# Attention and a long convolution mixed by a gate: when VectorE's lesser work may begin, the normalisation in three pieces, and other places for two sets of loads

## The chip, the core and the metric

The kernel runs on one core of one Trainium2 chip. The metric is device microseconds from the launch to the end of the program. Three engines matter here. TensorE (PE in the profile) multiplies, ScalarE (ACT) takes exponentials, VectorE (DVE) does everything else. SyncE (SP) issues nearly all transfers. Each engine works through its own queue strictly in the order in which the program wrote it, and waits on semaphores where an operand is not there yet.

## The reference

```python
def reference(A_x, A_wqkv, A_wo, B_u, B_A_re, ..., B_log_dt, B_Dskip, gate_w):
    g = sigmoid((x * gate_w).sum(-1, keepdims=True))
    # a: attention, 32 heads of 16, sequence 2048, no mask
    q, k, v = (x @ wqkv) split in heads
    a = softmax(q @ k.T * 16 ** -0.5) @ v @ wo
    # b: a diagonal state-space layer, 512 channels of 128 complex states
    K[d, l] = real(sum_n C[d, n] * exp(dt * A[d, n] * l) * dt * B[d, n])
    b = causal_convolution(x, K) + x * Dskip
    return g * a + (1 - g) * b          # (1, 2048, 512), bfloat16
```

## The kernel before

**The attention.** A block is four heads and a quarter of the queries (512), so there are 32 blocks, 0 to 31. A block has 16 key tiles of 128 keys, and each gives four score tiles, one for each head: 2048 score tiles of 128 keys by 512 queries in all. They are handled in 683 *groups* of three. The groups are numbered from 0 here, and group n is the n-th long ScalarE instruction `ET<-SC`. For each group TensorE multiplies `SC<-Qm,KT` into one of two score buffers (`SC0`, `SC1`, in turn), and ScalarE takes the exponential of it into seats of `ET`, a ring of 15 tiles. TensorE then multiplies these with the values (`OA<-ET,VE`).

**VectorE's share of the exponentials.** In some groups ScalarE takes only two of the three tiles. VectorE makes the third from the bits of a scaled score (`bits`, `DZ<-SC`). Four such tiles make a *set*, which is one key tile of four heads; 64 sets make 256 tiles. A set also needs two more VectorE steps over all four tiles, `DU<-DZ` and later `DZ<-DZ` in place, with products `OA<-DZ,VE`, `OA<-DU,VS` and `OA<-DZ,VS` between them. A block may only end once its sets' products are in.

**The end of a block.** `norm_a` transposes `OA` into `OT`. `norm_b` (one pair of blocks at a time) takes the reciprocal `Rz`, from block 24 on multiplies it by the gate `gq`, and multiplies it into `ON`. `norm_c` transposes `ON` into `OnT`, which the output product needs.

**The convolution** runs beside it, in pieces on VectorE and TensorE: tables of powers (`tt`, `PT`), the convolution's near part (`kstage`, `Kst`), states for each chunk of 64 steps (`sstage`, `SG`, marks S0 to S15 for its 16 channel blocks), a scan over the chunks, and 32 units of `y` (`ystage`, unit u marks `yu{u}`). A y unit reads `Py` and `Tt`, which `yload` fetches, and `XY`, which `xload` fetches. Its result goes through DRAM and comes back transposed as `Yl`. At the end `outs` adds `Yl` to the gated attention of the first three quarters, in three additions `AR<-AR,Yl`, and stores them. The last quarter goes through TensorE: `first` and the closing lines multiply `Yl` with the identity and `OnT` with `Wo` into one accumulator.

**The order.** A scheduler inside the kernel (`Sched`) decides in which order the instructions of each queue are written. Each piece of work is a thread that yields segments: an engine, a cost, and a rank `up`, where a smaller rank goes first. After each group, `fill(until, pe_until, want)` picks segments whose inputs it believes ready before `until`, the believed end of that group's exponential. Segments with rank -1 or -2 are those for which others wait at once: `bits`, `norm_a`, the emptying of the accumulator `MB`. On TensorE, `want` asks for a least amount of multiplying. Where real work does not reach it, products with zeros are written (`<-wm`). `force` pulls work ahead of its turn where a group cannot go on without it, for instance where the exponentials need a seat in `ET` that an earlier product still reads. For VectorE the only test of time before the change is this one (`e` is the believed start):

```python
                elif e > until:
                    continue
```

Every matmul is recorded in one helper, so the profile gives all of them line 626. Tiles tell them apart.

Of the kernel before, what the change touches and what calls it, by code (L numbers as in the profile page):

```python
# [18 lines left out]
T = 64  # L19
# [18 lines left out]
SGH = 256  # L38
SGAT = (175, 315)
SMM = .058  # L40
XS = 128 * DH ** -.5 / math.log(2)
STEP = ((42, 205 / 256), (84, 166 / 256))
XB = 128 * (127 - math.log2(3.15037))
# [236 lines left out]
class Sched:  # L280
# [89 lines left out]
    def fill(self, until, pe_until, want=0):  # L370
        while True:
            best = None
            for t in self.thr:
                e = self.est(t)
                if e is None:
                    continue
                if t.eng == "PE":
                    own = sum(a[2].get("a", 0) for a in t.seg if isinstance(a, tuple))
                    room = max(0, want - self.p.act - own) * ZCOL
                    if e + t.cost + room > pe_until and t.up > 0 or e > min(until, pe_until):  # L380
                        continue
                elif e > until:
                    continue
                now = self.p.tm[t.eng]
                k = (max(e, now + .3) if e > now + .02 else now, t.up, t.n)
                if best is None or k < best[0]:
                    best = (k, t)
            if best is None:
                return
            self.issue(best[1])  # L390
# [22 lines left out]
def declare(nc, es):  # L413
    B = {}

    def sb(name, free, dt=BF16):
        B[name] = Buf(name, "sb", free, dt)
# [83 lines left out]
        sb(f"X2{k}", 1024)  # L501
        sb(f"XY{k}", 32 * 64)

    sb("Py", 3 * 2 * 16 * T)
    sb("Tt", 3 * 8 * 64)
    sb("Yst", 4 * 256)
    sb("XR", 2 * 1024)
    for i in range(2):
# [101 lines left out]
def record(nc, p, B, ins):  # L610
# [369 lines left out]
    def norm_b(b, n=1):  # L980
        w = b % 2 + 1 - n
        at, ks = (lambda o, d, k: OT(512 * w + o, ([[512, 2]] if n == 2 else []) + d)), range(w, w + n)
        two = [[16, 2]] if n == 2 else []
        op("DVE", lambda v: v.reciprocal(Rz(16 * w, two + [[1, 16]]), at(16, [[32, 16]], 0)), [(OT, k, b - n + 1 + k - w) for k in ks],
           [(Rz, k) for k in ks], c=.25)
        if b >= 24:
            gq = B["gq"]
            op("DVE", lambda v: v.tensor_tensor(Rz(16 * w, two + [[1, 16]]), Rz(16 * w, two + [[1, 16]]), gq(0, ([[0, 2]] if n == 2 else []) + [[1, 16]]), ALU.mult),
               [(Rz, k) for k in ks] + [(gq, j) for j in range(4)], [(Rz, k) for k in ks], c=.11)
        op("DVE", lambda v: v.tensor_tensor(ON(16 * w, two + [[32, 16], [1, 16]]), at(0, [[32, 16], [1, 16]], 0),  # L990
                                            Rz(16 * w, two + [[1, 16], [0, 16]]), ALU.mult),
           [(OT, k, b - n + 1 + k - w) for k in ks] + [(Rz, k) for k in ks], [(ON, k) for k in ks], c=.08 + .267 * n)
# [290 lines left out]
    def sstage(blk):  # L1283
# [8 lines left out]
        for bank in range(4):  # L1292
            yield ("LOCK", "MB")
            kh, part = bank % 2, bank // 2
            for k0 in range(0, 8, 4):
                yield ("PE", 4 * SMM)
                for k in range(k0, k0 + 4):
# [3 lines left out]
                       [(Qt, (blk % 2, 2 * part + kh), blk)] + [(X2[blk % 4], 0, blk)], [(MB, 0, ('S', blk, bank))],  # L1301
                       c=SMM, a=64)
            yield ("DVE", .65, -1)
# [48 lines left out]
    Py, Tt, Yst, ytd, Yl = B["Py"], B["Tt"], B["Yst"], B["ytd"], B["Yl"]  # L1352
# [2 lines left out]

    def yload(u):
        blk, hf = divmod(u, 2)
        r = u % 3
        yield ("SP", .5)
        dma("SP", lambda e: e.dma_start(Py(r * YN, [[16 * T, 2], [1, 16 * T]]),  # L1360
                                        ptd.dram(blk * P * PTN + hf * 16 * T, [[PTN, P], [CB * T, 2], [1, 16 * T]])),
            [(ptd, blk)], [(Py, r, u)], c=.62, lat=3.8)
        for par in range(2):
            for a in range(2):
                yield ("SP", .4)
                dma("SP", lambda e, par=par, a=a: e.dma_start(
                    Tt(r * 512 + 256 * a, [[64, 4], [1, 64]], 64 * par, 64),
                    kpd.dram(blk * P * 8 * P + (2 * hf + a) * 40 * 8 * P + par * 9 * P, [[1, 64], [18 * P, 4], [1, 64]])),
                    [(kpd, blk)], [(Tt, (r, par, a), u)], c=.64, lat=2.8)
        sch.mark(f"yl{u}")  # L1370

    def yloads():
        yield ("AFTER", "S12")
        for u in range(2 * NBLK):
            if u >= 3:
                yield ("AFTER", f"yu{u - 3}")
            yield from yload(u)

    def ystage():
        def unit(u):  # L1380
            blk, hf = divmod(u, 2)
            qr, bl = divmod(blk, 4)
            sg, h, k8 = SG[qr // 2], qr // 2, blk % 8
            r, r2 = u % 3, u % 4
            yield ("AFTER", f"scan{h}")
            yield ("AFTER", "gt")
            yield ("AFTER", f"yl{u}")
# [84 lines left out]

    def xyloads():
        for qr in range(4):
            yield ("AFTER", f"yu{8 * qr - 5}" if qr else "S12")
            yield from xload(B[f"XY{qr}"], qr)
            sch.mark(f"xy{qr}")

# [35 lines left out]
    def wo_load(b):  # L1514
        load("SP", b, lambda: dap(ins["wo"], 0, [[D, P], [P * D, 4], [1, D]]), [(b, 0)], [[D, 4], [1, D]])
# [43 lines left out]
    def outs():  # L1559
        for blk in range(NBLK):  # L1560
            yield ("AFTER", f"yr{blk}")
        for qc in range(3):
            AO = B[f"AR{qc}"]
            yield ("DVE", 2.3, 0)
            op("DVE", lambda v, qc=qc, AO=AO: v.tensor_tensor(AO(0, [[D, 4]] + NAT), AO(0, [[D, 4]] + NAT), Yl(4 * D * qc, [[D, 4]] + PERM), ALU.add),  # L1565
               [(AO, r, "a") for r in range(4)] + [(Yl, x) for x in range(NBLK)], [(AO, r, "y") for r in range(4)], c=2.2)
            later("SP", .5, 3, lambda qc=qc, AO=AO: dma("SP", lambda e: e.dma_start(dap(ins["out"], 512 * qc * D, [[D, P], [P * D, 4], [1, D]]), AO(0, [[D, 4], [1, D]])),
                                                        [(AO, r, "y") for r in range(4)], [(B["d_out"], qc)], c=.5, lat=3))
        yield ("SP", .5)
        wo_load(B["Wo"])  # L1570
        sch.mark("outs")

    def projs():
# [28 lines left out]
    def norms():  # L1602
        for b in range(31):
            yield ("AFTER", f"end{b}")
            yield ("DVE", .75, -2)
            norm_a(b)
            sch.mark(f"n{b}")
            if b == 30:
                yield ("DVE", .65, 1)
                norm_b(b)  # L1610
            if b % 2 == 1:
                yield ("DVE", .9, 1)
                norm_b(b, 2)
                yield ("DVE", .7, 1)
                norm_c(b)
                sch.mark(f"c{b}")
# [93 lines left out]
    for g in range(NG):  # L1710
# [8 lines left out]
        if g + 1 < NG:  # L1719
# [5 lines left out]
            while lack >= 256 and bare:  # L1725
                n = 512 if lack >= 512 else 256
# [10 lines left out]
        t = p.tm["ACT"]  # L1737
# [5 lines left out]
        while lack >= 256 and p.tm["PE"] < t + OVER:  # L1743
# [4 lines left out]
            n = 512 if lack >= 512 else 256  # L1748
# [11 lines left out]
    ahead_of(1)  # L1760
    ahead_of(2)
    norm_a(31)
    norm_b(31)
    for k in range(2):
        norm_c(31, k, 2)
        for i in (2 * k, 2 * k + 1):
# [3 lines left out]
    for i in range(4):  # L1770
        b, off, sl = banks[i]
# [40 lines left out]
```

## Time and profile before

| | us |
|---|---|
| median of 3 runs | 840.84 (839.78 to 841.8) |
| the profiled execution | 841.1 |
| its span, first to last instruction | 839.3 |
| ScalarE busy | 818.9 (98%) |
| VectorE busy | 788.4 (94%) |
| TensorE busy | 696.9 (83%) |

ScalarE is busy nearly all the time. A group's exponential and the idle time ahead of it are the rows to read. In the timeline, a bracket at the end of a row holds the engine's idle time before the row and the instruction that ended it. The granted clock is the share of TensorE's full clock, 1.00 or 0.50 here.

### The profile page before, as it was taken

To read this page: it belongs to the slowest core of one execution; us is meant where nothing else is said; L and a number is where in the kernel's file an instruction comes from. 1 tells how busy PE (TensorE), PEld (TensorE's weight loads), DVE (VectorE), ACT (ScalarE), POOL (GpSimd) and SP (SyncE) were. 2 spreads that over 40 slices of the span, in tenths; PEclk is the share of its full clock that TensorE was granted. 3 is DMA by queue.
4 is the path that set the end of the run, shared out by engine and by line. 5 is a ranking of instruction groups with operands and counts; after the bars stand their busy time and mean duration, and the time that the engine had idled before them with its cause. 6 is when DMAs were issued, how large, how long until landed. Compare 5 with 4: busy or idle time off the path is not lost.

```text
span 839.3 us, 21027 instructions
## 1 busy us (share of the span) xinstructions
PE 696.9 (83%) x8977; PEld 253.4 (30%) x9002; DVE 788.4 (94%) x1344; ACT 818.9 (98%) x695; POOL 11.0 (1%) x13
## 2 busy tenths in 40 slices
PE   7787777778778888887787888789887889999987
PEld 3232332222212333332232332244432223444322
DVE  5799999998899999999999999999999989999996
ACT  7999999999999999999999999999999999999986
POOL 4000000000000000000000000000000000000000
PEclk9999999998999999999999999999999999999989
DMA  9650044792450789983392692066664025555113
GB/s 206 148 78 11 23 76 98 198 228 56 135 174 5 213 108 219 138 207 65 137 149 38 97 176 46 1 146 164 168 147 125 4 74 112 124 131 135 28 40 98
DMA packets 247954, 94.91 MB, mean 113 GB/s; under 512 B 222644, under 2 KB 234804, under 8 KB 245812
## 3 DMA queue, kind: packets, MB, share of 16 engines
q1 hardware_dynamic: 245988, 92.51, 50.1%
q10 hardware_dynamic: 1872, 1.05, 0.6%
q8 instruction: 71, 1.16, 0.5%
q14 instruction: 23, 0.19, 0.1%
HBM read 33.08 MB, written 35.01 MB: 81 GB/s over the span
## 4 chain that ended last, share of the span: by engine, by line
ACT 91%; PE 5%; DVE 2%; DMA 1%; issue 0%; ACTq 0%; DVEq 0%
ACT ET L907 91%; PE SC L626 2%; PE OA L626 2%; DMA Wk<-in_A_wqkv_dram 1%; DVE DZ L943 1%; PE MB L626 0%; DVE DZ L954 0%; DVE AR L1565 0%; DVE OT L978 0%; ACTq L630 0%; DVE Kst L1272 0%; DVE ON L990 0%; DVE OnT L997 0%; DVE KT L716 0%; DVE fo L1776 0%
## 5 line engine op out<-in xcount | busy, mean ns | idle before, releaser
L907 ACT ACTIVATE ET<-SC 128x1536 bf16<-128x1536 f32 (+1 forms) x683 | 810.6, 1545 | 8.4 <-PE SC L626 6.6
L626 PE MATMUL SC<-Qm,KT 32*128 32x512 bf16 x2048 | 279.1, 389 | 124.0 <-ACT ET L907 107.4
L626 PE MATMUL OA<-wm 128*32 128x512 bf16 (+3 forms) x1390 | 205.8, 369 | 1.2 <-DVE wm L679 1.2
L626 PE MATMUL OA<-ET,VE 128*32 128x512 bf16 x1792 | 180.8, 396 | 2.0 <-DVE OT L978 1.0
L943 DVE TENSOR_SCALAR DZ<-SC 128x512 uint16<-128x512 f32 x256 | 170.1, 683 | 9.5 <-PE SC L626 7.9
L626 PEld LDWEIGHTS SC<-Qm,KT 32*128 32x128 bf16 x2048 | 71.2, 91 | 341.5 <-ACT ET L907 300.6
L626 PEld LDWEIGHTS OA<-ET,VE 128*32 128x32 bf16 x1792 | 45.7, 93 | 104.0 <-issue 98.1
L626 PEld LDWEIGHTS OA<-wm 128*32 128x32 bf16 (+2 forms) x1390 | 55.3, 96 | 26.4 <-issue 17.7
L954 DVE TENSOR_SCALAR DZ<-DZ 128x2048 uint16<-128x2048 uint16 x64 | 44.0, 688 | 4.2 <-PE OA L626 4.1
L1304 DVE TENSOR_SCALAR SG<-MB 128x512 bf16<-128x512 f32 x64 | 43.6, 682 | 0.6 <-PE MB L626 0.2
L954 DVE TENSOR_SCALAR DU<-DZ 128x2048 uint16<-128x2048 uint16 x64 | 43.4, 686 | 0.1
L626 PE MATMUL MB<-X,Qt 128*128 128x64 bf16 x512 | 43.0, 244 | 0.0
L1339 DVE TENSOR_TENSOR G<-s,s 128x512 f32<-128x512 f32 x60 | 41.2, 687 | 1.0
L1331 DVE TENSOR_TENSOR s<-G,MU 128x512 f32<-128x512 f32 x60 | 41.1, 685 | 0.0
L1333 DVE TENSOR_TENSOR s<-G,MU 128x512 f32<-128x512 f32 x60 | 41.0, 683 | 0.0
L1336 DVE TENSOR_TENSOR s<-s,SG 128x512 f32<-128x512 f32 x60 | 40.9, 682 | 0.0
L626 PEld LDWEIGHTS MB<-X,Qt 128*128 128x128 bf16 x512 | 28.8, 116 | 20.3 <-issue 20.3
L1001 DVE TENSOR_TENSOR ft<-FP,L 128x1024 f32<-128x1024 f32 (+1 forms) x32 | 34.5, 1084 | 0.2
L1001 DVE TENSOR_TENSOR PT<-tt,tt 128x1024 bf16<-128x1024 bf16 x48 | 32.8, 683 | 0.5
L626 PEld LDWEIGHTS MB<-Py,SG 128*32 128x32 bf16 x1024 | 27.9, 167 | 6.4 <-issue 3.7
L626 PE MATMUL MB<-Py,SG 128*32 128x64 bf16 x1024 | 28.8, 231 | 0.0
L1342 DVE CAST SG<-G 128x512 bf16<-128x512 f32 x60 | 25.4, 423 | 1.2
(167 smaller groups left out, 607.7 us busy)
## 6 DMA issues: line engine op xcount, KB each, us to landing
gm_ptd<-PT SPq DMA_DIRECT2D x16, 1024.0 KB, 5.9
Py<-gm_ptd SPq DMA_DIRECT2D x32, 512.0 KB, 4.6
gm_kpd<-Kst SPq DMA_DIRECT2D x16, 256.0 KB, 3.8
Tt<-gm_kpd SPq DMA_DIRECT2D x128, 32.0 KB, 3.3
gm_xrd<-in_A_x_dram SPq DMA_DIRECT2D x1, 2048.0 KB, 13.4
gm_xcd<-wm SPq DMA_DIRECT2D x4, 512.0 KB, 10.3
gm_xcd<-XR SPq DMA_DIRECT2D x32, 64.0 KB, 1.9
Wo<-in_A_wo_dram SPq DMA_DIRECT2D x4, 512.0 KB, 4.2
```

What stands on the lines that cost most here:

```text
L626: op("PE", lambda t: t.matmul(out(), lhsT(), rhs(), start=start, stop=stop, skip_group_check=True, **kw), R, W, c=c, lat=.15, a=a, cfg=cfg)
L907: op("ACT", lambda a: a.activation(ET(512 * e, [[1, 512 * n]]), sc(0, [[1, 512 * n]]), AF.Exp, scale=DH ** -0.5), [(sc, i, g) for i in ran ...
L943: op("DVE", lambda v: v.tensor_scalar(z.u16(512 * k, [[1, 512 * n]]), sc(512 * na, [[1, 512 * n]]), XS, XB, ALU.mult, ALU.add), [(sc, na + ...
L954: op("DVE", lambda v: v.tensor_scalar(t.u16(0, [[1, 2048]]), z.u16(0, [[1, 2048]]), float(STEP[k][0]), None, ALU.add), R, W, c=.07 + 2048 ...
L1001: op(eng, lambda v: v.tensor_tensor(o(), a(), b_(), f), R, W, c=c)
L1304: op("DVE", lambda v, kh=kh, part=part: v.tensor_scalar(sg(2 * SGH + SGH * part + CB * k8 + 16 * kh, [[2 * SGH, 32], [1, 16]]), MB(0, [[16 ...
L1331: op(e, lambda v: v.tensor_tensor(s2(0, W), G(0, W), MU(d0, [[0, 2], [1, 256]]), ALU.mult), key("G", "MU"), [(s2, 0)], c=F5)
L1333: op(e, lambda v: v.tensor_tensor(s3(0, W), G(256, [[-256, 2], [1, 256]]), MU(D + d0, [[D, 2], [1, 256]]), ALU.mult), key("G", "MU") + [(M ...
L1336: op(e, lambda v, so=so: v.tensor_tensor(s2(0, W), s2(0, W), sg(so, [[SGH, 2], [1, 256]]), ALU.add), [(s2, 0)] + ks, [(s2, 0)], c=F5)
L1339: op(e, lambda v: v.tensor_tensor(G(0, [[1, 512]]), s2(0, [[1, 512]]), s3(0, [[1, 512]]), ALU.add), [(s2, 0), (s3, 0)], [(G, 0)], c=F5)
L1342: op(e, lambda v, so=so: v.tensor_copy(sg(so, [[SGH, 2], [1, 256]]), G(0, W)), key("G"), ks if c < NCH - 2 else [(sg, k, (h, 'G')) for k i ...
```

## The change

Five edits, none of which adds or removes an instruction on VectorE, ScalarE or SyncE:

```diff
+YR = 4
+DOV = .8
...
-                elif e > until:
+                elif e > until or t.eng == "DVE" and t.up > -1 and e + min(t.cost, 1.) > until + DOV:
                     continue
...
-    sb("Py", 3 * 2 * 16 * T)
-    sb("Tt", 3 * 8 * 64)
+    sb("Py", YR * 2 * 16 * T)
+    sb("Tt", YR * 8 * 64)
...
+        yield ("DVE", .25, 1)
         op("DVE", lambda v: v.reciprocal(Rz(...
         if b >= 24:
             gq = B["gq"]
+            yield ("DVE", .11, 1)
             op("DVE", lambda v: v.tensor_tensor(Rz(...
+        yield ("DVE", .08 + .267 * n, 1)
         op("DVE", lambda v: v.tensor_tensor(ON(...
...
-        r = u % 3
+        r = u % YR
...
-        yield ("AFTER", "S12")
+        yield ("AFTER", "S15")
         for u in range(2 * NBLK):
-            if u >= 3:
-                yield ("AFTER", f"yu{u - 3}")
+            if u >= YR:
+                yield ("AFTER", f"yu{u - YR}")
...
-            yield ("AFTER", f"yu{8 * qr - 5}" if qr else "S12")
+            yield ("AFTER", f"yu{8 * qr - 5}" if qr else "S15")
...
+        yield ("SP", .5)
+        wo_load(B["Wo"])
         for qc in range(3):
             AO = B[f"AR{qc}"]
             yield ("DVE", 2.3, 0)
...
-        yield ("SP", .5)
-        wo_load(B["Wo"])
...
-                yield ("DVE", .9, 1)
-                norm_b(b, 2)
+                yield from norm_b(b, 2)
```

First, a VectorE segment of rank 0 or more is only written if its believed end (at most 1 us of its cost counts) lies within 0.8 us of the end of the current exponential. Second, `norm_b` is three segments instead of one, so that other work may stand between them. Third, the rings for `Py` and `Tt` have four places instead of three. Fourth, the first loads into them and into `XY` begin after S15 instead of S12. Fifth, the last load of `Wo` is issued ahead of the three additions instead of behind them. Since the scheduler decides everything one piece at a time, the order on all queues differs from about group 120 on. The number of sets stays 64, and ScalarE gets the same exponentials. TensorE gets 33 instructions fewer, all of them products with zeros.

The first place is VectorE's queue at the first set (`DZ_57`), near 243 us in the profile before. Before:

```order
L943 TENSOR_SCALAR DZ_57<-SC 128x512
L1272 CAST Kst<-MB 128x8x64
L1273 TENSOR_SCALAR Kst<-MB,Dp 128x8
L978 STREAM_TRANSPOSE OT<-OA 128x512
L943 TENSOR_SCALAR DZ_57<-SC 128x512
L1272 CAST Kst<-MB 128x8x64
L1273 TENSOR_SCALAR Kst<-MB,Dp 128x8
L984 RECIPROCAL Rz<-OT 128x32
L990 TENSOR_TENSOR ON<-OT,Rz 128x2x16x16
L943 TENSOR_SCALAR DZ_57<-SC 128x512
L997 STREAM_TRANSPOSE OnT_75<-ON 128x512
L943 TENSOR_SCALAR DZ_57<-SC 128x512
```

And with the change, at the same place of the same queue:

```order
L1277 CAST Kst<-MB 128x8x64
L1278 TENSOR_SCALAR Kst<-MB,Dp 128x8
L980 STREAM_TRANSPOSE OT<-OA 128x512
L987 RECIPROCAL Rz<-OT 128x32
L995 TENSOR_TENSOR ON<-OT,Rz 128x2x16x16
L1277 CAST Kst<-MB 128x8x64
L1278 TENSOR_SCALAR Kst<-MB,Dp 128x8
L945 TENSOR_SCALAR DZ_57<-SC 128x512
L1002 STREAM_TRANSPOSE OnT_75<-ON 128x512
L945 TENSOR_SCALAR DZ_57<-SC 128x512 x3
```

The set begins three groups later (group 174 instead of 171), and the two `Kst` pairs, `OT`, `Rz` and `ON` stand ahead of its first step instead of between its steps.

The second place is TensorE's queue where the gate's products are made (`MB<-gwT,xT`), near 183 us before; `<-wm` are the products with zeros. Before:

```order
L626 MATMUL SC<-Qm,KT 128x512 x2
L626 MATMUL OA<-ET,VE 32x512 x4
L626 MATMUL MB<-gwT,xT 128x1 x8
L626 MATMUL SC<-Qm,KT 128x512 x3
L626 MATMUL OA<-ET,VE 32x512 x4
L626 MATMUL MB<-gwT,xT 128x1 x8
L626 MATMUL SC<-Qm,KT 128x512 x3
L626 MATMUL MB<-gwT,xT 128x1 x8
L626 MATMUL SC<-wm 32x512 x4
```

With the change:

```order
L628 MATMUL OA<-ET,VE 32x512 x4
L628 MATMUL MB<-gwT,xT 128x1 x8
L628 MATMUL OA<-wm 32x512 x8
L628 MATMUL SC<-Qm,KT 128x512 x3
L628 MATMUL OA<-ET,VE 32x512 x4
L628 MATMUL MB<-gwT,xT 128x1 x8
L628 MATMUL SC<-Qm,KT 128x512 x3
L628 MATMUL SC<-wm 32x512 x4
L628 MATMUL SC<-Qm,KT 128x512 x3
```

Three groups in a row had no `OA<-wm 32x512` before; now two have none, and the group ahead of them has eight.

The third place is VectorE's queue at the three additions, near 807 us before. Before:

```order
L1565 TENSOR_TENSOR AR_80<-AR_80,Yl 128x2048
L978 STREAM_TRANSPOSE OT<-OA 128x512
L943 TENSOR_SCALAR DZ_73<-SC 128x512
L984 RECIPROCAL Rz<-OT 128x16
L988 TENSOR_TENSOR Rz<-Rz,gq 128x16
L990 TENSOR_TENSOR ON<-OT,Rz 128x16x16
L943 TENSOR_SCALAR DZ_73<-SC 128x512 x2
L943 TENSOR_SCALAR DZ_67<-SC 128x512 x3
L1565 TENSOR_TENSOR AR_83<-AR_83,Yl 128x2048
L943 TENSOR_SCALAR DZ_67<-SC 128x512
L1565 TENSOR_TENSOR AR_86<-AR_86,Yl 128x2048
L954 TENSOR_SCALAR DZ_69<-DZ_69 128x2048
```

With the change:

```order
L1572 TENSOR_TENSOR AR_80<-AR_80,Yl 128x2048
L992 TENSOR_TENSOR Rz<-Rz,gq 128x16
L945 TENSOR_SCALAR DZ_67<-SC 128x512
L995 TENSOR_TENSOR ON<-OT,Rz 128x16x16
L945 TENSOR_SCALAR DZ_69<-SC 128x512 x4
L1572 TENSOR_TENSOR AR_83<-AR_83,Yl 128x2048
L1572 TENSOR_TENSOR AR_86<-AR_86,Yl 128x2048
L956 TENSOR_SCALAR DZ_71<-DZ_71 128x2048
L956 TENSOR_SCALAR DU_68<-DZ_67 128x2048
L956 TENSOR_SCALAR DU_70<-DZ_69 128x2048
L956 TENSOR_SCALAR DZ_73<-DZ_73 128x2048
L956 TENSOR_SCALAR DZ_67<-DZ_67 128x2048
```

The additions stand in groups 670, 676 and 677 instead of 663, 669 and 672. The second and third now follow all `DZ<-SC` of the program, back to back, with six steps over whole sets still behind them (the five shown and `DZ_69<-DZ_69`).

More of the change, by code (lines that the diff above doesn't have):

```diff
@@ L1383, in unit @@
             sg, h, k8 = SG[qr // 2], qr // 2, blk % 8
-            r, r2 = u % 3, u % 4
+            r, r2 = u % YR, u % 4
             yield ("AFTER", f"scan{h}")
@@ L1608, in norms @@
             if b == 30:
-                yield ("DVE", .65, 1)
-                norm_b(b)
+                yield from norm_b(b)
             if b % 2 == 1:
-                yield ("DVE", .9, 1)
-                norm_b(b, 2)
+                yield from norm_b(b, 2)
                 yield ("DVE", .7, 1)
@@ L1762, in record @@
     norm_a(31)
-    norm_b(31)
+    list(norm_b(31))
     for k in range(2):
```

## The prediction

> **What bounds the kernel now.** The page comes first: the span, each engine's share, and the chain that ended last.
>
> ```profile
> span 839.3 us, 21027 instructions
> PE 696.9 (83%) x8977; PEld 253.4 (30%) x9002; DVE 788.4 (94%) x1344; ACT 818.9 (98%) x695; POOL 11.0 (1%) x13
> ACT 91%; PE 5%; DVE 2%; DMA 1%; issue 0%; ACTq 0%; DVEq 0%
> ```
>
> The chain is ScalarE for 91%, so the program is one row of exponentials, and a change helps only where ScalarE stands idle or behind the last exponential. The groups by form say how the exponentials divide, and the number of each form stays as it is:
>
> ```profile
> L907 ACT ACTIVATE ET<-SC 128x1536 bf16<-128x1536 f32 x426 | 583.5, 1764 | 4.0 <-PE SC L626 2.7 <-PE OA L626 1.2
> L907 ACT ACTIVATE ET<-SC 128x1024 bf16<-128x1024 f32 x257 | 250.5, 1182 | 4.4 <-PE SC L626 4.0 <-PE OA L626 0.2
> ```
>
> So 8.4 us of idle time lie ahead of exponentials. ScalarE's timeline says where (start, time taken, then the idle time in brackets):
>
> ```profile
> 15.08 155.91 ACT L907 ACTIVATE ET<-SC 128x1536 bf16<-128x1536 f32 x116
> 168.81 21.01 ACT L907 ACTIVATE ET<-SC 128x1536 bf16<-128x1536 f32 x15
> 190.75 2.84 ACT L907 ACTIVATE ET<-SC 128x1536 bf16<-128x1536 f32 x2 [0.93 <-PE SC L626]
> 195.48 1.45 ACT L907 ACTIVATE ET<-SC 128x1536 bf16<-128x1536 f32 x1 [0.45 <-PE SC L626]
> 197.09 50.79 ACT L907 ACTIVATE ET<-SC 128x1536 bf16<-128x1536 f32 x39 [0.15 <-PE SC L626]
> 248.69 1.94 ACT L907 ACTIVATE ET<-SC 128x1024 bf16<-128x1024 f32 x2 [0.82 <-PE SC L626]
> 250.80 1.02 ACT L907 ACTIVATE ET<-SC 128x1024 bf16<-128x1024 f32 x1 [0.17 <-PE SC L626]
> 252.27 1.02 ACT L907 ACTIVATE ET<-SC 128x1024 bf16<-128x1024 f32 x1 [0.45 <-PE SC L626]
> 254.22 6.39 ACT L907 ACTIVATE ET<-SC 128x1536 bf16<-128x1536 f32 x5 [0.92 <-PE SC L626]
> 747.86 62.48 ACT L907 ACTIVATE ET<-SC 128x1536 bf16<-128x1536 f32 x64 [1.25 <-PE OA L626]
> 811.87 2.06 ACT L907 ACTIVATE ET<-SC 128x1024 bf16<-128x1024 f32 x2 [1.54 <-PE SC L626]
> 814.17 1.02 ACT L907 ACTIVATE ET<-SC 128x1024 bf16<-128x1024 f32 x1 [0.24 <-PE SC L626]
> 815.70 15.22 ACT L907 ACTIVATE ET<-SC 128x1024 bf16<-128x1024 f32 x13 [0.51 <-PE SC L626]
> ```
>
> Four stretches hold nearly all of it: 0.93 + 0.45 + 0.15 = 1.53 us near 190, 0.82 + 0.17 + 0.45 + 0.92 = 2.36 us near 250, 1.25 us at 747.86, and 1.54 + 0.24 + 0.51 = 2.29 us near 812. A wait can also hide in an instruction's own time. A group of three takes (155.91 - 1.45) / 115 = 1.343 us, from the first row and the 1.45 us of one alone; the 15 from 168.81 should take 14 x 1.343 + 1.45 = 20.25 us and took 21.01. The first stretch thus cost 1.53 + 0.76 = 2.29 us. A group of two takes 1.94 - 1.02 = 0.92 us.
>
> The windows view gives the granted clock around the first and the last of these stretches (after the sum: busy time of PE, PEld, DVE, ACT, POOL, then the clock):
>
> ```profile
> 182.79:186.20 3.41, 2.56 (x40) 1.14 (x37) 3.31 (x5) 3.41 (x4) 0.00 (x0) 1.00 1.01 398
> 186.20:196.44 10.24, 9.59 (x96) 2.74 (x93) 6.78 (x15) 8.87 (x8) 0.00 (x0) 0.50 0.38 84
> 807.42:810.84 3.42, 1.89 (x26) 0.59 (x18) 3.35 (x6) 2.92 (x4) 0.00 (x0) 1.00 0.22 73
> 810.84:817.67 6.83, 6.82 (x48) 1.24 (x44) 6.30 (x9) 4.96 (x5) 0.00 (x0) 0.50 0.12 40
> ```
>
> In both, 3.4 us in which TensorE was busy for less than usual are followed by half the clock, and the score products then come too late for ScalarE.
>
> **The change part by part.** No count changes on ScalarE or VectorE, so every term is a wait that goes or comes. I take them in the order of time, against the profiled execution's 841.1 us, which lies 0.26 us above the median of the three runs; I leave that difference alone.
>
> *The gate's products, near 190: -2.3 us.* The stretch holds no wait for VectorE. Three groups with eight `gwT` products each and no zero products stood together, and the clock was halved behind them. In the new order only two such groups stand together, and the one before them has eight zero products. The trace of before does not show what two do; the bounds are 0 and -2.29. I take the whole, because two groups last 2 x 1.343 = 2.7 us, less than the 3.41 us of the window that preceded the fall.
>
> Here the Trainium skill, "TensorE: Matmul & The Clock Gate", section "Part 1: The HAM clock gate", says that the clock falls to one half after at least one idle window of about 3.4 us, and that this window runs free of the kernel's start. The length agrees with this trace (3.41 and 10.24 us are one and three of them). The condition does not: TensorE was busy for 2.56 of the 3.41 us ahead of the fall. By the page's words a few zero products more or fewer decide nothing, this term would be 0, and the sum 840.2.
>
> *The first set, near 250: -2.1 us.* VectorE's timeline there:
>
> ```profile
> 246.37 0.68 DVE L1272 CAST Kst<-MB 128x512 bf16<-128x512 f32 x1
> 247.09 0.25 DVE L1273 TENSOR_SCALAR Kst<-MB,Dp 128x8 bf16<-128x8 f32 x1
> 247.23 0.34 DVE L984 RECIPROCAL Rz<-OT 128x32 f32<-128x32 f32 x1
> 247.60 0.69 DVE L990 TENSOR_TENSOR ON<-OT,Rz 128x512 bf16<-128x512 f32 x1
> 248.21 0.68 DVE L943 TENSOR_SCALAR DZ<-SC 128x512 uint16<-128x512 f32 x1
> ```
>
> Four lesser instructions, 248.21 - 246.37 = 1.84 us of them, stand ahead of a `DZ<-SC` in groups that last only 0.92 us; the score product for that buffer waits for it, then ScalarE, and the thin stretch is followed by half the clock. In the new order all of this stands ahead of the set's first `DZ<-SC`, in groups 171 to 173, which have three ScalarE tiles. There it fits: two `Kst` pairs, `OT`, `Rz` and `ON` are at most 2 x 0.93 + 0.70 + 0.34 + 0.69 = 3.6 us (0.70 us is the time of an `OT`, below) against 3 x 1.343 = 4.0. Only `OnT` (about 0.7) still stands between the first two `DZ<-SC`. The bounds are 0, if `Kst` comes late from TensorE, and -2.36; I leave 0.3 of it for `OnT`.
>
> *The rule for lesser work and the pieces of `norm_b`* have no price of their own: an instruction costs what it cost before, and VectorE has 839.3 - 788.4 = 50.9 us without work to take up what is put off. What they do is in these places.
>
> *The seats of the ring and the additions: -0.6 us.* VectorE's timeline:
>
> ```profile
> 746.47 0.69 DVE L954 TENSOR_SCALAR DZ<-DZ 128x2048 uint16<-128x2048 uint16 x1 [0.62 <-PE OA L626]
> 806.88 2.28 DVE L1565 TENSOR_TENSOR AR<-AR,Yl 128x2048 bf16<-128x2048 bf16 x1
> 809.07 0.71 DVE L978 STREAM_TRANSPOSE OT<-OA 128x512 f32<-128x512 f32 x1
> 809.71 0.65 DVE L943 TENSOR_SCALAR DZ<-SC 128x512 uint16<-128x512 f32 x1
> 814.82 2.28 DVE L1565 TENSOR_TENSOR AR<-AR,Yl 128x2048 bf16<-128x2048 bf16 x1
> 817.62 2.28 DVE L1565 TENSOR_TENSOR AR<-AR,Yl 128x2048 bf16<-128x2048 bf16 x1
> 820.42 1.89 DVE L954 TENSOR_SCALAR DU<-DZ 128x2048 uint16<-128x2048 uint16 x3
> 828.49 0.69 DVE L954 TENSOR_SCALAR DZ<-DZ 128x2048 uint16<-128x2048 uint16 x1 [0.77 <-PE OA L626]
> 830.11 0.69 DVE L954 TENSOR_SCALAR DZ<-DZ 128x2048 uint16<-128x2048 uint16 x1 [0.93 <-PE OA L626]
> 831.54 0.72 DVE L978 STREAM_TRANSPOSE OT<-OA 128x512 f32<-128x512 f32 x1 [0.73 <-PE OA L626]
> ```
>
> At 747.86 the exponential of group 603 wanted seats of `ET` that a product still read, and that product stood behind the last step of a set, which began at 746.47: 1.39 us from step to exponential. In the new order this wait is gone at 603 and comes at 667 and, behind an `OT`, at 219. At 667 the step follows two `DZ<-SC` of group 665, about 0.4 us into group 666, so the wait is 0.4 + 1.39 - 0.92 = 0.9. At 219 I take 0.4, between 0 and the 1.25 of group 603.
>
> The first addition blocks VectorE for 2.28 us. Before, the `DZ<-SC` behind it began 809.71 - 806.88 = 2.83 us after it, and ScalarE lost 1.54, and 0.24 + 0.51 more at half the clock. The new order has `Rz` (at most 0.34) instead of `OT` between them, which is about 0.4 shorter, and the wait at 667 has let VectorE catch up by some tenths. I take 0.9 + 0.75 = 1.65, between 0 (the second addition, at 814.82, made no wait that a row shows) and 2.29. The other two now follow the last `DZ<-SC`, and no exponential waits for them. Here then: 0.9 + 0.4 + 1.65 = 2.95 against 1.25 + 2.29 = 3.54.
>
> *The last block's end: +1.3 us.* Before, the third addition ended at 819.90, the last exponential at 815.70 + 15.22 = 830.92, and the last `OT` began 0.62 us later. In the new order six groups of three and one of two remain when the second addition is due, 6 x 1.343 + 1.02 = 9.1 us; some 0.4 us for the last `DZ<-SC` and 4.56 us for two additions leave 4.1. Six steps over whole sets follow. Three take 1.89 us, so the fourth begins 2.2 us ahead of the last exponential's end. Before, from the fifth to `OT` it was 831.54 - 828.49 = 3.05 us, and from the fifth to the sixth 1.62, with VectorE waiting for TensorE between them. At that pace `OT` would begin 1.62 + 3.05 - 2.2 = 2.5 us behind the last exponential, 1.9 later than before. At VectorE's own pace it would be no later. I take 1.3: the two rows show waits for TensorE, but one of its products may be done sooner here.
>
> *The loads: 0.*
>
> ```profile
> Wo<-in_A_wo_dram SPq DMA_DIRECT2D x4, 512.0 KB, 4.2
> 743.74 2.57 SPq L1366 DMA_DIRECT2D Tt<-gm_kpd  x4
> 826.85 0.39 PE L626 MATMUL MB<-Wo,OnT 128*128 128x512 bf16 x1
> ```
>
> The last `Wo` is now on its way ten groups ahead of the product that reads it, over 9 us against 4.2. Issued behind the additions it would land about when the last exponential ends, and the `MB<-Wo,OnT` products, which now stand in group 677, would block TensorE's queue: the edit covers what the later additions would have cost. The first loads for y become 22 transfers in a row on SyncE, at 2.57 / 4 = 0.64 us each 14 us, behind group 397. The first y unit stands in group 426, and the queries of block 20, which are queued behind the transfers, are used in group 425, at least 28 x 0.92 = 26 us later. With four places a load starts one unit sooner; no row shows a y unit waiting for one. If that cover went, a unit would wait for a landing of some 4 us, and the exponentials with it.
>
> *What I cannot see: +0.5 us.* The whole order is new from group 120 on, and the trace of before has small waits in places where nothing special stands.
>
> The sum is 841.1 - 2.3 - 2.1 - 0.6 + 1.3 + 0.5 = 837.9.
>
> **The rivals.** *The clock falls at the gate's products all the same.* For it: two groups without zeros may still fill most of a window, which may begin anywhere. Against it: the eight zero products ahead. ScalarE then loses the 2.29 us as before, at 837.9 + 2.3 = 840.2. By the page's rule above the time is this one too, though for another reason.
>
> *The waits only move.* VectorE is busy for 94%, and what is put off has to be done; each late `DZ<-SC` that is avoided comes back at a block's end, as at group 667. Against it: the two largest stretches of late `DZ<-SC` have their causes named and moved. Then the time is 841.1. The same would come out if the rule seldom changed anything, but the first place shows that it does.
>
> *More time at half the clock: slower.* TensorE has 33 zero products less, and each remaining wait, at 219, 667 and 670, makes a thin window. Near 190, 10.24 us at half the clock cost 2.29 us, 0.22 for each. With 4.9 / 0.22 = 22 us more at half the clock than I count, the time is 0.2% over the one before; at 23 us more, three such stretches less a part, it is 843. Against it: a wait near 812 was followed by 6.83 us only, at (0.24 + 0.51) / 6.83 = 0.11 for each.
>
> **How the numbers follow.** My forecast has a chance of 0.48, the clock at the gate's products 0.18, waits that only move 0.14, more half clock 0.20. About 0.2%, 1.7 us, is what a measurement of this kernel can tell from no change. The forecast's own range is 835.8 (the end, `OnT` and what I cannot see cost nothing: 1.3 + 0.3 + 0.5 less) to 839.6 (the first set gains only 0.4); nearly all of it is faster by more than 0.2%, and a little of the second case, so 0.50. The rest of the second case and the third make 0.30, the last 0.20. The range over all cases runs from 835.8 to 842.8, which leaves out a part of the last case and a little below.
>
> **What would show it.** Right: the granted clock stays at 1.00 from 180 to 250 us; the first set passes without a bracket over 0.3; one wait near group 667 and one behind the first addition, together 2 to 3 us; the last `OT` begins 1.5 to 2.5 us behind the last exponential. Wrong: half clock near 190; brackets of over 1 us at places that I have not named; or a last `OT` more than 3 us late, which would mean that the additions reached into the end.

## The result, and the profile after

The changed kernel takes 846.26 us (median of 4, 845.65 to 846.94) against 840.42 us for the one before (median of 4): 1.0067 of it, 95% interval 1.005 to 1.0085. It is slower, by about 5.7 us. I had forecast 837.9.

The page of the changed kernel, with the span, the engines' shares and the chain that ended last:

```profile
span 844.4 us, 20984 instructions
PE 703.9 (83%) x8969; PEld 253.3 (30%) x8969; DVE 786.3 (93%) x1344; ACT 819.4 (97%) x695; POOL 11.0 (1%) x13
ACT 76%; DVE 12%; PE 7%; DMA 4%; issue 1%; SPq 0%; ACTq 0%; DVEq 0%
```

ScalarE is as busy as before (819.4 us against 818.9), but the chain runs through it for 76% only and not for 91%. It now passes through VectorE and through transfers. The timeline of ScalarE says where it stands idle (start, time taken, idle time ahead in brackets):

```profile
151.34 1.45 ACT L909 ACTIVATE ET<-SC 128x1536 bf16<-128x1536 f32 x1 [2.74 <-PE SC L628]
153.41 16.22 ACT L909 ACTIVATE ET<-SC 128x1536 bf16<-128x1536 f32 x12 [0.62 <-PE SC L628]
172.40 28.84 ACT L909 ACTIVATE ET<-SC 128x1536 bf16<-128x1536 f32 x21 [2.77 <-PE SC L628]
202.16 1.45 ACT L909 ACTIVATE ET<-SC 128x1536 bf16<-128x1536 f32 x1 [0.92 <-PE SC L628]
252.87 2.79 ACT L909 ACTIVATE ET<-SC 128x1536 bf16<-128x1536 f32 x2 [0.81 <-PE SC L628]
255.91 1.02 ACT L909 ACTIVATE ET<-SC 128x1024 bf16<-128x1024 f32 x1 [0.24 <-PE SC L628]
257.42 3.13 ACT L909 ACTIVATE ET<-SC 128x1024 bf16<-128x1024 f32 x3 [0.49 <-PE SC L628]
815.98 6.53 ACT L909 ACTIVATE ET<-SC 128x1024 bf16<-128x1024 f32 x7 [0.69 <-PE OA L628]
822.82 1.94 ACT L909 ACTIVATE ET<-SC 128x1024 bf16<-128x1024 f32 x2 [0.30 <-PE SC L628]
825.43 9.25 ACT L909 ACTIVATE ET<-SC 128x1536 bf16<-128x1536 f32 x7 [0.68 <-PE SC L628]
```

The two largest waits, 2.74 us at group 101 and 2.77 us at group 114, are new. The trace of before had one unbroken row there. They lie ahead of group 120, from which the order of the queues differs much. In VectorE's and TensorE's queues some neighbours are exchanged earlier too (between 73 and 84 us, and near 131 us), while SyncE's transfers stand in the same order up to 164 us. The releaser named is TensorE, and behind TensorE stands VectorE, and behind VectorE a transfer. The same moments in VectorE's and TensorE's timelines:

```profile
148.97 0.69 DVE L718 CAST Qs<-MB 128x512 bf16<-128x512 f32 x1 [3.98 <-DMA gm_qd<-Qs]
149.72 1.03 PE L628 MATMUL MB<-xT,Wq 128*128 128x512 bf16 x2 [3.02 <-DVE Qs L718]
164.59 0.43 DVE L1227 COPY PT<-B 128x1024 bf16<-128x1024 bf16 x1 [1.45 <-DMA gm_ptd<-PT]
167.35 0.43 DVE L1227 COPY PT<-B 128x1024 bf16<-128x1024 bf16 x1 [2.33 <-DMA gm_ptd<-PT]
170.77 1.03 PE L628 MATMUL MB<-xT,Wq 128*128 128x512 bf16 x2 [3.05 <-DVE Qs L718]
```

VectorE wants to overwrite a seat of `Qs`, later a piece of `PT`, which a store to DRAM has not read yet. TensorE's next `MB` product waits for VectorE, and since its queue is in order, so do the score products behind it. Why are the stores late? Here are four rows of SyncE's queue, first of the kernel before:

```profile
99.28 0.34 SPq L1597 DMA_DIRECT2D gm_qd<-Qs  x1
99.66 3.46 SPq L1455 DMA_TRANSPOSE XR<-gm_xrd  x2
132.50 2.11 SPq L1597 DMA_DIRECT2D gm_qd<-Qs  x2
146.85 0.92 SPq L1239 DMA_DIRECT2D gm_ptd<-PT  x2
```

and the same four of the changed kernel:

```profile
99.72 0.34 SPq L1602 DMA_DIRECT2D gm_qd<-Qs  x1
113.95 2.55 SPq L1460 DMA_TRANSPOSE XR<-gm_xrd  x2
146.96 1.05 SPq L1602 DMA_DIRECT2D gm_qd<-Qs  x2
160.57 0.93 SPq L1244 DMA_DIRECT2D gm_ptd<-PT  x2
```

The list of SyncE's waits between 98 and 115 us (total, times, longest) names what it waited for, and VectorE's timeline has that operation:

```profile
SPq L263 <- DVE nwi L1006: 13.8, 1, 13.8
```

```profile
113.20 0.68 DVE L1006 TENSOR_TENSOR nwi<-u,u 128x512 bf16<-128x512 f32 x1
```

Both reach 99.7 us together. Then the changed kernel waits 13.8 us before its first load of `XR`, and all that follows is some 14 us late: 113.95 - 99.66 = 14.3, 146.96 - 132.50 = 14.5, 160.57 - 146.85 = 13.7. The operation that makes `nwi` has nothing to do with `XR`. It is the last to read `u3`, a tile of the table of powers. The kernel's own code chooses the addresses in SBUF once the order stands. These are the bytes within each partition and the groups in which a tile is in use, as that code gives them:

```
        before                           changed
u3      45248-47296,   groups 12-74      77696-79744,  groups 12-74
XR      167296-171392, from group 81     77696-81792,  from group 81
```

The larger rings take 4,096 and 1,024 bytes more for each partition. The placement tries many orders of all tiles and keeps the one that needs the least, so two larger tiles gave nearly every tile another address (138 of 141). `XR` came to lie on `u3`. By the group numbers of the program that is free of charge, 81 being behind 74. On the chip SyncE runs ahead of its place in the program: its first `XR` load started at 99.66 us, about (99.66 - 11.35) / 1.343 = 66 groups after the first exponential at 11.35 us, and the last read of `u3`, in group 74, ends at 113.20 + 0.68 = 113.88.

### The profile page after: what moved, and what is told of

Read it like the earlier page. It is cut to its first block, busy times and chain, and to the rows that moved or that the text cites. A ratio compares the mean times of both kernels' runs of the same rounds, so it can differ in the third digit from the quotient of the medians.

```text
span 844.4 us, 20984 instructions
## 1 busy us (share of the span) xinstructions
PE 703.9 (83%) x8969; PEld 253.3 (30%) x8969; DVE 786.3 (93%) x1344; ACT 819.4 (97%) x695; POOL 11.0 (1%) x13
## 4 chain that ended last, share of the span: by engine, by line
ACT 76%; DVE 12%; PE 7%; DMA 4%; issue 1%; SPq 0%; ACTq 0%; DVEq 0%
ACT ET L909 76%; DVE tt L1006 3%; PE SC L628 3%; DMA gm_ptd<-PT 3%; PE OA L628 2%; DVE PT L1006 2%; DVE ft L1006 2%; PE MB L628 1%; DVE DZ L945 1%; DMA Wk<-in_A_wqkv_dram 1%; DVE DZ L956 1%; DVE B L1006 1%; DVE OT L980 0%; DVE Qs L718 0%; DVE FP L1006 0%
## 5 line engine op out<-in xcount | busy, mean ns | idle before, releaser
L628 PE MATMUL OA<-DZ,VS 128*32 128x512 bf16 x256 | 25.3, 385 | 1.3 <-DVE DZ L956 1.2
```

The source lines that it names most:

```text
L628: op("PE", lambda t: t.matmul(out(), lhsT(), rhs(), start=start, stop=stop, skip_group_check=True, **kw), R, W, c=c, lat=.15, a=a, cfg=cfg)
```

## The experiments

Each kernel is compared with the one before on the same chip.

**e1, the same instructions at other addresses.** The order on every queue is that of the changed kernel. For the placement, `XR` counts as in use from 25 groups before its first load.

```diff
+LEAD = {'XR': 25}
...
+    early = {b: b.first - LEAD.get(b.name, 0) for b in sbs}
-            busy = sorted((o.lo, o.hi) for o in done if o.first <= b.last + 1 and b.first <= o.last + 1)
+            busy = sorted((o.lo, o.hi) for o in done if early[o] <= b.last + 1 and early[b] <= o.last + 1)
```

> The changed kernel with every instruction in the same order, but the addresses in SBUF chosen so that XR, the ring into which SP loads from about 100 us on, shares no bytes with a tile that is read after group 56 (the placement counts XR as live from 25 groups before its first use). Theory A, addresses: the change's larger rings made the placement put XR on the bytes of u3, whose last reader is the nwi operation of VectorE near 113.2 us; SP's queue waits there 13.8 us and all that SP issues up to 165 us is late. Then XR's first load starts near 99.7 us again, the waits of ScalarE of 2.7 us at groups 101 and 114 are gone, and the time is 846.3 - 7.7 = 838.6 us (837 to 840.5). Theory B, order: the rule for lesser work and the pieces move VectorE's work so that SP's stores come late; addresses do not matter: 846 us, both waits stay. Theory C, larger rings cost something of their own: 846 us.

Measured: 839.01 us, 0.9973 of before (0.996 to 0.9986). SyncE's load and ScalarE's timeline:

```profile
99.84 3.26 SPq L1462 DMA_TRANSPOSE XR<-gm_xrd  x2
99.23 90.94 ACT L911 ACTIVATE ET<-SC 128x1536 bf16<-128x1536 f32 x67
190.86 5.48 ACT L911 ACTIVATE ET<-SC 128x1536 bf16<-128x1536 f32 x4 [0.68 <-PE SC L630]
```

One row of 67 exponentials stands where the two waits were. Addresses alone turned 1.0067 into 0.9973; theories B and C are out.

**e2, the wait alone, on the kernel before.** Its own order and its own addresses, with one dependence more:

```diff
+        if b.name == "XR":
+            b.over.append(bufs["u3"])
```

> The kernel before, with its own order and its own addresses, and one dependence added: SP's first load of XR also waits until the last reader of u3 is done, as it has to in the changed kernel. Theory A: SP waits some 13 us near 100 us, waits of ScalarE of some 2 to 3 us appear near groups 101 and 114, and the time is 840.4 + 4 to 8 = 844 to 848 us. Theories B and C: the wait has slack and the time stays at 840.4 us (within 1 us).

Measured: 849.89 us, 1.0092 (1.0078 to 1.0105). SyncE's wait, then ScalarE's timeline:

```profile
SPq L261 <- DVE nwi L1003: 13.8, 1, 13.8
```

```profile
151.17 1.45 ACT L909 ACTIVATE ET<-SC 128x1536 bf16<-128x1536 f32 x1 [2.63 <-PE SC L628]
171.66 1.45 ACT L909 ACTIVATE ET<-SC 128x1536 bf16<-128x1536 f32 x1 [3.34 <-PE SC L628]
```

The same 13.8 us, the same two places (groups 101 and 113), and a loss of 0.92% of 841.8, 7.7 us. The time is above theory A's 844 to 848 us, the loss inside its 4 to 8 us. With e1 this is shown from both sides.

**e3, the rings alone** (`YR = 4`, S15; this placement happens to leave `XR` free).

```diff
+YR = 4
...
-    sb("Py", 3 * 2 * 16 * T)
+    sb("Py", YR * 2 * 16 * T)
...
-        yield ("AFTER", "S12")
+        yield ("AFTER", "S15")
```

> Of the change only the rings of four and the later permission for their loads (S15); the rest is as before. The placement that comes out keeps XR free of bytes that are read later than group 56. Theory A: no wait near groups 101 and 114, and 840.4 us within 1.5 (the prediction had the rings at no price by themselves). Theory C: the larger rings cost by themselves, 843 to 846 us. Theory B: 840.4 us.

Measured: 841.1 us, 0.9998 (0.9987 to 1.0009). Where `XR` is free, the rings have no price of their own that shows.

**e4, the change without its rings** (`YR = 3`, S12; here too `XR` is free).

```diff
-YR = 4
+YR = 3
...
-        yield ("AFTER", "S15")
+        yield ("AFTER", "S12")
```

> The change without its rings: rings of three and loads allowed from S12 as before, but the rule for lesser work, the pieces and the earlier last weights as in the changed kernel. The placement that comes out keeps XR free. Theory A: no waits at groups 101 and 114, 837 to 841 us (the forecast's sum without its term for the ring seats: about 838.5). Theory B: 845 to 847 us with the two waits. Theory C: 838 to 841 us.

Measured: 846.81 us, 1.0058 (1.0041 to 1.0075). No theory had this: the time is B's, but the waits at 101 and 114 are gone, as A says, and others stand at groups 478 to 487. ScalarE's and TensorE's timelines there:

```profile
615.75 3.01 ACT L909 ACTIVATE ET<-SC 128x1024 bf16<-128x1024 f32 x3 [1.72 <-PE SC L628]
622.76 1.45 ACT L909 ACTIVATE ET<-SC 128x1536 bf16<-128x1536 f32 x1 [0.90 <-PE SC L628]
614.74 0.64 PE L628 MATMUL MB<-Py,SG 128*32 128x64 bf16 x24 [2.09 <-DMA Py<-gm_ptd]
621.13 0.37 PE L628 MATMUL MB<-Py,SG 128*32 128x64 bf16 x8 [0.69 <-DMA Py<-gm_ptd]
```

The y units wait for `Py`, and the scores queue behind them. A reading is that three places are too few in the order that the rest of the change makes; e9 tests it.

**e9, ring or permission?** The changed kernel with `XR` free as in e1, rings of four, but S12:

```diff
-        yield ("AFTER", "S15")
+        yield ("AFTER", "S12")
```

> The changed kernel with rings of four but the first loads allowed from S12 as before, XR at a place of its own. e4 (rings of three, S12) lost about 5 us near groups 477 to 487, where TensorE waited for Py. Theory F: three places are too few for y's units in the order that the change gives; with four the wait is gone and the time is that of e1, 0.996 to 0.9985 of before. Theory G: it is the early permission; then the loss stays, 1.003 to 1.007.

Measured: 838.84 us, 0.9976 (0.9964 to 0.9988), with no wait over 0.2 us between groups 330 and 660. Theory F: it is the fourth place. S15 against S12 makes no difference that shows.

**e5, e6, e7: e1 without one of its other edits** (the rule; the pieces; the earlier weights).

```diff
-                elif e > until or t.eng == "DVE" and t.up > -1 and e + min(t.cost, 1.) > until + DOV:
+                elif e > until:
```

> The change without its rule for lesser work (rings of four, the pieces and the earlier last weights stay), XR at a place of its own. Theory D: it is the rule that takes late bits of scores out of the way and so gives the gain that e1 showed (0.27%); without it the time is that of before, 0.998 to 1.002 of it, with waits near groups 130 to 135 and 175 to 180 together over 2 us and a third addition well ahead of the last exponential (tail of 8.4 us behind it). Theory E: pieces, rings and weights give the gain: 0.996 to 0.998 of before.

```diff
...
-                yield from norm_b(b, 2)
+                yield ("DVE", .9, 1)
+                norm_b(b, 2)
...
```

> The change without the pieces: norm_b is one segment again, the rule, the rings and the earlier weights stay, XR at a place of its own. Theory D: the same gain as in e1, 0.996 to 0.9985 of before. Theory E: with whole segments the rule puts long pieces off, and the gain is gone: 0.999 to 1.002.

```diff
-        yield ("SP", .5)
-        wo_load(B["Wo"])
         for qc in range(3):
...
+        yield ("SP", .5)
+        wo_load(B["Wo"])
```

> The change with the last weights issued behind the three additions, as before, XR at a place of its own. The additions now end only near the last exponential, so by the prediction's words the weights land late, the products with them block TensorE, and the end is later than in e1 by 1 to 4 us (0.9985 to 1.002 of before). Rival: the products that read them are late anyway behind the last sets, and the time is that of e1 (0.997 of before).

Measured: 0.9975 (0.9961 to 0.9989), 0.9989 (0.9977 to 1.0001) and 0.9995 (0.998 to 1.0011), against e1's 0.9973.

e5 has theory E's time, but it differs from e1 by more than the rule. Its page counts 65 sets, where the kernel before, the changed one and e1 have 64:

```profile
L910 ACT ACTIVATE ET<-SC 128x1536 bf16<-128x1536 f32 (+1 forms) x683 | 808.9, 1556 | 9.0 <-PE OA L629 4.7
L957 DVE TENSOR_SCALAR DU<-DZ 128x2048 uint16<-128x2048 uint16 x65 | 44.1, 685 | 0.1
```

Without the rule the scheduler gave VectorE one more set. Four groups thus have two ScalarE tiles instead of three, which by the usual steps of 1.333 and 0.903 us saves 4 x 0.43 = 1.7 us, 0.2% of the time and most of e5's gain. Against that, the idle time ahead of exponentials is 9.0 us, and 5.6 in e1, while e5 needs less time behind its last exponential (8.29 us against 9.76). So these runs do not show that the rule is worth nothing; what it is worth by itself stays open.

In e6's profile the four waits at the first set are back (0.82 + 0.16 + 0.35 + 0.92 = 2.25 us, in e1 0.19), and the time behind the last exponential is 10.89 us. Pieces and weights may each carry a part of the gain, but the intervals of e6 and e7 overlap e1's, so how the 0.27% divides stays open. For e7 the profiled execution does not show the late weights that I had expected: its `MB<-Wo,OnT` products ran at 822.62 and 824.59 us, with no wait for a transfer. But this execution, 838.06 us, was the fastest of twelve with a median of 841.95, so it does not tell what the others lost.

**e8, e1 with the additions in halves.** e1 still needed 838.10 - 828.34 = 9.76 us behind its last exponential (before: 839.31 - 830.93 = 8.38), and had waits of 0.29, 0.98 and 0.56 us at groups 674 to 679.

```diff
-            yield ("DVE", 2.3, 0)
-            op("DVE", lambda v, ...: v.tensor_tensor(AO(0, [[D, 4]] + NAT), ...), ..., c=2.2)
+            for hh in (0, 2):
+                yield ("DVE", 1.2, 3)
+                op("DVE", lambda v, ...: v.tensor_tensor(AO(hh * D, [[D, 2]] + NAT), ...), ..., c=1.13)
```

> The changed kernel with XR at a place of its own, and each of the three additions in two halves of rank 3, which now stand between the last steps over the sets instead of ahead of them. Behind the last exponential e1 needed 9.8 us, before 8.4. If it is the two additions ahead of the six last steps that make the last block's end late (the prediction's term of +1.3), the end comes 1 to 1.7 us sooner than in e1: 0.9955 to 0.9965 of before, with the last OT about 0.6 us behind the last exponential. Rival: TensorE sets the pace of these steps, and the time is that of e1 (0.997).

Measured: 835.01 us, 0.9924 (0.9908 to 0.9939), the fastest of all: it beats both kernels, by more than I had expected. VectorE's timeline at the end of e1's order, here in the changed kernel:

```profile
824.74 4.49 DVE L1572 TENSOR_TENSOR AR<-AR,Yl 128x2048 bf16<-128x2048 bf16 x2
829.14 0.69 DVE L956 TENSOR_SCALAR DZ<-DZ 128x2048 uint16<-128x2048 uint16 x1
829.75 1.29 DVE L956 TENSOR_SCALAR DU<-DZ 128x2048 uint16<-128x2048 uint16 x2
836.67 0.72 DVE L980 STREAM_TRANSPOSE OT<-OA 128x512 f32<-128x512 f32 x1 [0.73 <-PE OA L628]
```

and in e8, with ScalarE's last long row:

```profile
815.27 0.68 DVE L958 TENSOR_SCALAR DZ<-DZ 128x2048 uint16<-128x2048 uint16 x1
815.87 1.29 DVE L958 TENSOR_SCALAR DU<-DZ 128x2048 uint16<-128x2048 uint16 x2
817.74 2.35 DVE L1575 TENSOR_TENSOR AR<-AR,Yl 128x1024 bf16<-128x1024 bf16 x2
820.61 2.35 DVE L1575 TENSOR_TENSOR AR<-AR,Yl 128x1024 bf16<-128x1024 bf16 x2
825.35 0.72 DVE L982 STREAM_TRANSPOSE OT<-OA 128x512 f32<-128x512 f32 x1 [0.65 <-PE OA L630]
807.50 17.34 ACT L911 ACTIVATE ET<-SC 128x1024 bf16<-128x1024 f32 x16 [0.69 <-PE OA L630]
```

Four of the six steps over the sets now go ahead of the remaining additions, and the other two stand between them. The last `OT` starts 825.35 - 824.84 = 0.5 us behind the last exponential instead of 836.67 - 834.68 = 2.0 (in the changed kernel). The time behind the last exponential is 833.13 - 824.84 = 8.29 us, 1.5 less than in e1, as I expected. More came from the first addition: only half of it, 1.22 us instead of 2.28, still stands among the bits of scores, and the 16 exponentials from 807.50 on follow without a wait. Halving and the lower rank came together here; which of them does it is not tested apart.

**e10 and e11, the halves without the rule, and on the kernel before.** e10 is e8 with the rule's line as before (e5's edit). e11 is the kernel before with e8's halves and the weights ahead of the additions, `XR` free.

> e8 (additions in halves of rank 3) without the rule for lesser work; rings, pieces and earlier weights stay, XR at a place of its own. e5 showed that without the rule the time is that of e1, within its interval. Theory H: the rule is worth nothing here either, and the time is that of e8, 0.991 to 0.994 of before. Theory I: halves need the rule, which keeps them out of the groups in which bits of scores are due; then 0.995 to 0.998.

> The kernel before with only two edits: the additions in halves of rank 3 and the last weights ahead of them; XR at a place of its own. Before lost 2.3 us near 812 behind the first addition. Theory H: the waits near groups 667 to 671 are gone or below 1 us and the end is no later: 0.995 to 0.998 of before. Theory I: 0.999 to 1.002.

Measured: 0.9972 (0.9957 to 0.9987) and 0.9981 (0.9969 to 0.9992), against e8's 0.9924. Theory I has e10's time: without the rule most of the gain of the halves is gone. ScalarE's timeline of e10, then that of e8 over the same groups:

```profile
748.26 1.94 ACT L910 ACTIVATE ET<-SC 128x1024 bf16<-128x1024 f32 x2 [1.22 <-PE OA L629]
790.77 1.94 ACT L910 ACTIVATE ET<-SC 128x1024 bf16<-128x1024 f32 x2 [1.33 <-PE OA L629]
```

```profile
733.93 66.46 ACT L911 ACTIVATE ET<-SC 128x1024 bf16<-128x1024 f32 x68
```

These two waits, 2.55 us, are not in e8. But like e5, e10 has 65 sets, so the runs show what comes of taking out the rule, one more set included. e10's profiled execution also waited 0.9 + 1.9 us near the gate's products, a place that differs between executions (last section), so the two waits are not the whole difference of the two profiles. e11 lies at the upper edge of theory H's interval and gains less than half of what e8 does; a wait of 1.18 us remains at group 669, more than theory H allowed.

**e12, a control:** the kernel before with e1's edit, so other addresses and nothing else.

> A control: the kernel before, every instruction in its order, other addresses for most tiles, XR again on bytes that nothing reads after group 56. If addresses matter only where SyncE meets a late reader, the time is that of before within 0.15%. If the choice of addresses matters by itself, it is off by more.

Measured: 842.28 us, 1.0014 (1.0001 to 1.0027). Another placement without the wait on `u3` is within 0.15% as expected, with little room; a cost of addresses by themselves of up to a quarter per cent is not excluded.

## Why the prediction was wrong

To compare, I add up by stage what each group's step takes over the usual 1.333 us (three tiles) or 0.903 (two), from one profiled execution each:

| place (groups) | forecast | changed - before | e1 - before |
|---|---|---|---|
| waits at 101 and 114 (95 to 119) | 0 | +7.5 | 0.0 |
| gate's products (120 to 139) | -2.3 | -1.5 | -1.0 |
| first set (168 to 181) | -2.1 | -0.5 | -2.3 |
| ring seats, additions (210 to 224, 595 to 611, from 640) | -0.6 | -1.7 | -0.4 |
| last block's end | +1.3 | +1.4 | +1.4 |
| all other places | +0.5 | -0.1 | +1.1 |
| sum | -3.2 | +5.1 | -1.2 |

**The step that failed is "The loads: 0".** It priced the transfers and when their places come free, and not the bytes that the larger rings take. Nothing in the order of the queues or in the trace of before shows an address; only the placement of the new program does, and since the kernel's code computes it, it could have been read beforehand. In place of the 0, the waits at groups 101 and 114 cost 7.5 us in the changed kernel's profile, and the same wait alone cost the kernel before 7.7 us (e2). "What I cannot see", +0.5, was argued from an order that is "new from group 120 on"; the loss lay ahead of that, where the order is nearly the same. None of the three rivals held this either. The slower one had another cause and came out at 843. Two of the signs that I had listed as proving me wrong, "brackets of over 1 us at places that I have not named" and "half clock near 190", are what the trace shows.

**The gate's products: sign right, reason wrong.** I had the clock stay at 1.00. It was halved again, in the changed kernel and in e1 (windows view; behind the span of each stretch the busy times of PE, PEld, DVE, ACT, POOL, then the granted clock):

```profile
192.79:196.20 3.41, 2.08 (x34) 0.74 (x31) 3.41 (x6) 3.41 (x4) 0.00 (x0) 1.00 0.69 158
196.20:203.03 6.83, 6.83 (x78) 2.21 (x70) 5.52 (x11) 5.92 (x5) 0.00 (x0) 0.50 0.69 281
184.36:191.19 6.83, 6.67 (x60) 1.64 (x57) 6.76 (x10) 6.11 (x6) 0.00 (x0) 0.50 0.77 304
```

So the first rival's mechanism held here, at a smaller loss than its 2.29 us. My mistake was to take one execution's stretch of half clock as a property of the order. Profiles of the old order lost 1.53 us of idle time here (before), 0.93 (e12) or none in any row (e2, e3). Those of the new order lost 0.92 (changed), 0.68 (e1), 0.71 (e8), 0.91 (e9) or none (e7).

**The first set: right where nothing disturbs it.** In e1, with the changed order, one bracket of 0.19, at 244.98 us, stands in place of the four of 2.36 us:

```profile
244.98 18.18 ACT L911 ACTIVATE ET<-SC 128x1536 bf16<-128x1536 f32 x16 [0.19 <-PE SC L630]
```

In the profiled execution of the changed kernel itself, waits of 0.81, 0.24 and 0.49 us came around a stretch of half clock from 250.8 us on. Both have the same order there, so the difference is not the order's. Still, this term is one of the order: the profiles of the old order (before, e2, e3, e12) have 2.1 to 2.6 us in these brackets, and those of the new one 1.54 (changed), 0.61 (e7) and 0.15 to 0.19 (e1, e8, e9).

**The ring's seats, the additions and the end: the places right, the sizes in part.** The wait at group 667 came (0.69 us idle, forecast 0.9), waits of 0.30 and 0.68 us follow behind the first addition (forecast 1.65 in all, found 0.98), and the one at 747.86 us is gone. The one named at 219 shows no bracket; the steps of groups 216 and 217 are 0.7 us longer than usual (forecast 0.4). The waits at 667 and behind the addition, which were to be 2 to 3 us together, are 1.67 in the changed kernel and 0.69 + 0.29 + 0.98 + 0.56 = 2.52 in e1. The last `OT` began 2.0 us behind the last exponential (forecast 1.5 to 2.5), and the end came 1.4 us later (forecast 1.3).

Without the wait on `u3` the change is worth -0.27% (-0.40 to -0.14), and my sum was -3.2 / 841.1 = -0.38%. That the two are so near is in part luck: e1's profile gains 1.2 us by these stages and not 3.2, and the gate's term was no property of the order. The first set, the additions and the end hold in kind. What the sum lacked is a term of some 7.5 us.

## What to carry to other kernels

When a change makes a tile larger or longer-lived, and a placement decides addresses, list for each tile that a transfer fills who last read its bytes, and compare that with when the *queue* gets there, not with the place in the program: a queue that runs ahead turns a free reuse into a wait of everything behind it. A wait that appears far from the edit, ahead of where the order changes, points there; the same instructions at other addresses, and the wait alone on the old kernel, decide it in two runs. And edits can depend on each other: the rest of the change needed the fourth place of the ring (e4 against e9), and the halves of the additions brought their full gain only with the rule (e8 against e10). Before an edit to a scheduler is called one edit, count the instructions of each form: without the rule there were 65 sets, not 64.

## What the runs showed of the hardware

SyncE reached its first `XR` load 15 groups ahead of its place in the program (99.66 us, group 66 against 81). A single wait of 13.8 us in that queue delayed the transfers behind it by 14 us for at least 47 us (113.95 to 160.57), and this cost ScalarE about 7.5 us in two places.

The stretches of half clock fall differently in executions of one and the same order. e12 has the order of the kernel before, whose clock was 0.50 for 10.24 us from 186.20 us on; in e12, and in the 73.9 us around this place in e7, which has the order of the changed kernel there, the windows view gives:

```profile
182.00:187.31 5.31, 3.79 (x61) 1.66 (x58) 5.21 (x7) 5.31 (x5) 0.00 (x0) 1.00 1.02 382
187.31:190.73 3.42, 3.42 (x31) 0.76 (x31) 3.39 (x7) 2.56 (x2) 0.00 (x0) 0.50 0.45 77
170.00:243.90 73.90, 53.63 (x678) 16.42 (x675) 66.62 (x111) 73.56 (x57) 0.52 (x1) 1.00 0.51 128
```

The Trainium skill, "TensorE: Matmul & The Clock Gate", section "Part 1: The HAM clock gate", says that the window by which the clock is judged is free-running. These traces fit it, since one order gave 10.24 and 3.42 us here, but no run shows the window itself. The time goes with the clock. Over 35 executions of the kernel before on one chip the mean granted clock lay between 0.981 and 0.991 and the time between 839.1 and 843.4 us, shorter with a higher clock. A straight line through span and clock gives 3.7 us for each 0.01 (2.9 over the 12 of e1, 3.0 to 3.3 over other sets of the kernel before, up to 5.2 in e10). A mean lower by 0.01 is 2% of the span, 16.8 us, at half clock, so each such us goes with 0.17 to 0.31 us; the prediction had 0.22 from one stretch. This does not separate cause from effect, since a wait that costs time also leaves TensorE with less to do. The means of the kernels order themselves alike: before 0.986, e1 0.990, e8 0.996. A profile of one execution tells what such a stretch costs, but not that it will be there.
